# ELU between the Strassen units: the second product of one token half moves forward, the other half's parts go through DRAM

## The chip, the core and the metric

The kernel runs on one core of a Trainium2 chip. The core has a matrix engine (PE, with its weight loader PEld), a vector engine (DVE), a scalar engine (ACT), a general engine (POOL) and a queue that issues DMAs (SP). Each engine works through its own list of instructions in order; an instruction waits until the semaphores it needs are set. The metric is the device time of one execution in microseconds (us), the median of several.

## The reference

Three stages follow each other. Batch 4, 8 heads, 576 positions, width 64 give 2304 tokens of 512 numbers, all in float32.

```python
out = attention_on_4x_pooled_rows(q, k, v)      # repeated four times along the sequence
out += attention_in_a_band(q, k, v)             # |i - j| < 4
x = out as 2304 x 512
h = x @ w_in                                    # 512 x 2048
g = np.where(h > 0, h, np.exp(np.minimum(h, 0)) - 1)   # ELU
x = g @ w_out                                   # 2048 x 512
a = x @ w_gate                                  # 512 x 1536
y = (a / (1 + np.exp(-a))) * (x @ w_val)        # x @ w_val: 512 x 1536
return y @ w_o2                                 # 1536 x 512
```

## The kernel before

Every float32 operand of a large product is split into a leading part and a rest ("hi" and "lo"); `products` then runs three matmuls (hi by hi, hi by lo, lo by hi), lines 994 to 996. The hi part is an ACT copy (line 1178), the lo part a subtraction on DVE or POOL (line 1175); `split_into` adds both.

The first MLP takes 1440 tokens in five chunks of 288 directly. The last 864 tokens are two halves of 432, and their first product is written with the seven products of a Strassen (Winograd) scheme, in 8 *units* (one per 256 of the 2048 columns). A unit is 7 products of 6 matmuls of 432 columns: 42 matmuls. `add_seven` keeps three PSUM banks (Z, E, B) for a unit; ACT copies four results out (line 1204), DVE adds three more to those copies (line 1207), and a later product of the unit accumulates in a bank only after its copy. A unit yields the 256 columns of h for both halves.

`add_last` runs this part. Before the change it works in two passes. First all 8 units: the results of a unit (`De`, `Do`, named `blk`) are stored to DRAM (`yd1`, line 1356). Then, for each half and each pair of column blocks, they are loaded again (`y`, line 1369), put through ELU (negative part on ACT or DVE, lines 1374 and 1376; exponential on ACT, line 1379; minus one and maximum on DVE, line 1380), split, and multiplied by `w_out`: 12 matmuls of 432 columns per 128 columns, 24 per unit and half. The four accumulators of a half hold four PSUM banks.

The weights of a unit are built by `add_weight_unit`: four sums of blocks and up to eight splits. Its buffers are `wu` (two of them, each as large as a whole unit) or, for every third unit of the first MLP, four small ones (`wt`). The second MLP (`add_second`) has the same units with 512 columns, three token groups and two kinds (`gate`, `val`) for six pairs of column blocks; its POOL also multiplies gate by value (`blk`), and prepares the weights of the last product (`add_output_weights`: tiles `t`, `oh`, stored to `od`).

The order of the program is not written out. A planner (`Work`) gets each step with its engines, its cost, what it reads and writes, and a due time; it plays the engines in time and lets each free engine take the ready step that is due first. Most numbers in the class-like block of constants are due times or offsets of due times. A step emitted is fixed: the engines then follow that order, whatever the real durations are.

Of the kernel before, what the change touches and what calls it, by code (L numbers as in the profile page):

```python
# [9 lines left out]
F32 = mybir.dt.float32  # L10
F32R = mybir.dt.float32r
# [3 lines left out]
AF = mybir.ActivationFunctionType  # L15
# [121 lines left out]
class Work:  # L137
# [5 lines left out]
    SECOND = 34.88  # L143
# [158 lines left out]
def attention_moe_moe(ctx: ExitStack, tc: tile.TileContext, q, k, v, w_in, w_out, w_gate, w_val, w_o2, ident_in, mask_in, band_in, picks_in, out):  # L302
# [80 lines left out]
    STEP2 = 7.62  # L383
    START = 37.63
    STEP0 = 4.81
    STEP = 4.49
    FIRST = -40.0
    VALUES = -46.28
    LATER = 113.73
    POOLED = -0.58  # L390
    EARLY = 3.56
    PREFER = -31.24
    EAGER = 27.32
    URGENT = 26.59
    FREE = 21.5
    SLACK = 0.0
    LOAD = 32.85
    KEEP0 = 2.05
    KEEP1 = 4.5
    DIRECT = 2, 3, 1  # L400
    PARTS1 = 32.94
    UNIT1 = -3.64
    LAG1 = 4.87
    PARTS = 10.49
    OUT = -4.36
    SUMS = 12.13
    SUMS3 = 2.56
    SECOND2 = 15.47
    LATE = 54.53
    AWAY0 = 2.17  # L410
    AWAY1 = 5.67
    LO1 = 16.02
    HI1 = 5.93
    LO2 = 26.91
    HI2 = 34.0
    LO3 = 32.37
    HI3 = 34.82
    KEYS = 29.3
    POOL1 = -0.72
    POOL0 = 19.72  # L420
    POOL2 = 10.16
    LOCAL = 3.95
    ROWS = 20.24
    INPUT = -2.49
# [43 lines left out]
    def add_words(due, raw, u, reads=()):  # L468

        def size():  # L470
            nc.scalar.activation(u.t.bitcast(F32), raw.t[:, :, 1].bitcast(F32), AF.Prelu, scale=2.0 ** -BIAS, alpha=MINUS)

        def rest():
            nc.scalar.activation(raw.t[:, :, 0], raw.t[:, :, 0].bitcast(U32), AF.Copy, bias=TOP3[1], scale=TOP3[0])

        def words():
            t = u.t.bitcast(I32)
            nc.vector.scalar_tensor_tensor(
                out=t, in0=t, scalar=3, op0=ALU.logical_shift_left, in1=raw.t[:, :, 0], op1=ALU.bitwise_or)
# [3 lines left out]
        return add("dve", 0.64, due - 2.5, words, reads=[raw, u, *reads], writes=[u])  # L483

    def add_weights(keys, dues, whole):

        made = {}
        for n, key in enumerate(keys):
# [18 lines left out]
            low = add(("act", "dve"), (0.67, 0.7), due - 4, rest, reads=[raw, w.whole], writes=[w], second=3.0)  # L507
# [660 lines left out]
    def both_cost(engines, n):  # L1168
        return tuple(0.16 + n * 0.00104 if e == "dve" else 0.06 + n * 0.0023 for e in engines)
# [60 lines left out]
    def add_direct(key, due, to, buf, after, more=()):  # L1230
# [18 lines left out]
        add("dve", 1.18, due - 2.5, words, reads=[raw, buf], writes=[buf])  # L1249
# [15 lines left out]
    def add_weight_unit(kind, j, due, after, whole):  # L1265

        engines = EITHER if kind == "in" else PO
        u, s, w = gens.new([P, 4, HT], name="u"), gens.new([P, 4, HT], name="s"), Unit(kind == "in" and j % 3 == 2)
# [27 lines left out]
    PROD1 = 6 * 0.1964  # L1296
# [21 lines left out]
    def add_last(opened, exps, closed, made):  # L1318
# [20 lines left out]
        yd1 = [pools["dram"].tile([P, 2, TS], F32, tag=f"y1_{j}", name="yd1") for j in range(NJ1)]  # L1339
        ws, stored_h, after, pes1 = [], {}, opened, []  # L1340
        for j in range(NJ1):
            start = base + 7 * PROD1 * j
# [3 lines left out]
            De, Do = (gens.new([P, 2, HS], name="blk") for _ in range(2))  # L1346

            def emit(m, ps, first, w=w):
                a = AT[m]
                for k in range(2):  # L1350
# [4 lines left out]
                             [(De, 0), (De, 1), (Do, 0), (Do, 1)], HS, None, w)  # L1355
            stored_h[j] = [add("sp", 0.5, start + 7 * PROD1 + 2, lambda j=j, par=par, D=D: nc.sync.dma_start(
                out=yd1[j][:, par], in_=D.t.rearrange("p h c -> p (h c)")), reads=[D], after=[*done[2 * par], *done[2 * par + 1]], nbytes=P * TS * 4)
                for par, D in ((0, De), (1, Do))]
            pes1.append([t for x2 in xs.values() for b in x2 for t in b.readers if "pe" in t.costs][-7:])
        base += 7 * PROD1 * NJ1  # L1360
        ran = []
        for h in range(2):
            acc = [banks.new(lambda: range(8)) for _ in range(NP)]
            after2 = []
            for j in range(NJ1):
                due = base + 24 * 0.1964 * (j + NJ1 * h)
                Y, E = (gens.new([P, 2, HS], name="y1") for _ in range(2))
                gs = [slot(h_slots) for _ in range(2)]
                add("sp", 0.5, due - 12 - LAG1, lambda j=j, h=h, Y=Y: nc.sync.dma_start(out=Y.t, in_=yd1[j][:, :, h * HS:(h + 1) * HS]),
                    writes=[Y, E], nbytes=P * 2 * HS * 4, after=[*stored_h[j], *(ran[-4] if len(ran) > 3 else pes1[(-3, -2, -2, -1)[len(ran)]])])  # L1370

                def negative(engine, Y=Y, E=E):
                    if engine == "act":
                        nc.scalar.activation(E.t, Y.t, AF.Relu, scale=-1.0)
                    else:
                        nc.vector.tensor_scalar(out=E.t, in0=Y.t, scalar1=-1.0, scalar2=0.0, op0=ALU.mult, op1=ALU.max)  # L1376

                add(COPIER, (0.92, 1.0), due - 8 - LAG1, negative, reads=[Y], writes=[E], second=3)
                last_exp = [add("act", 0.92, due - 7 - LAG1, lambda E=E: nc.scalar.activation(E.t, E.t, AF.Exp, scale=-1.0), reads=[E], writes=[E])]
                add("dve", 1.06, due - 6 - LAG1, lambda Y=Y, E=E: nc.vector.scalar_tensor_tensor(  # L1380
                    out=Y.t, in0=E.t, scalar=-1.0, op0=ALU.add, in1=Y.t, op1=ALU.max), reads=[Y, E], writes=[Y])
                for par, g in enumerate(gs):
                    split_into(EITHER, due - 5 - LAG1, lambda g=g: g.t[:, 0], lambda g=g: g.t[:, 1], lambda Y=Y, par=par: Y.t[:, par], [Y], [g], [g], HS)

                    def gemm2s(h=h, j=j, par=par, g=g, acc=acc):
                        wo = wt["out", 2 * j + par]
                        if (h, j, par) == (1, NJ1 - 1, 1):
                            over.append(1)
                        for i in range(NP):
                            cs = slice(i * P, (i + 1) * P)  # L1390
                            products(acc[i].t[:, :HS], (wo.t[:, 0, cs], wo.t[:, 1, cs]), (g.t[:, 0], g.t[:, 1]), j + par == 0, j + par == NJ1)

                    n = 2 * j + par
                    after2.append(add("pe", 12 * 0.1964, due + 2.36 * par, gemm2s, reads=[wt["out", n], g], writes=acc,
                                      after=after2[-1:] if n == NF1 - 1 else [*after2[:1], *after2[-2:-1]]))
                ran.append(after2[-1:])
            x2s = pools["dram"].tile([P, NP, HS], F32, tag=f"x2_{NC + h}", name="x2d")
            put = []
            for i in range(NP):
                t = gens.new([P, HS], name="o1")  # L1400
                add(COPIER, (0.55, 0.6), due + 5, lambda engine, i=i, t=t, acc=acc: copy(engine, t.t, acc[i].t[:, :HS]), reads=[acc[i]], writes=[t], second=0)
                put.append(add("sp", 0.5, due + 6, lambda i=i, t=t, x2s=x2s: nc.sync.dma_start(out=x2s[:, i], in_=t.t), reads=[t], nbytes=P * HS * 4))
            segments.append((TP + h * HS, TP + (h + 1) * HS, x2s, put))
        return last_exp, [*ws[-1].made.values()], pes1[-1], base + 2 * NF1 * 12 * 0.1964
# [31 lines left out]
    def add_second(opened, exps, closed, base, behind):  # L1436
        xs, tokens = {}, {}
        for g, (t0, T) in enumerate(groups):
# [3 lines left out]
            for h, (s0, n) in enumerate(halves):  # L1442
                pieces = [(max(s0, a) - s0, min(s0 + n, z) - s0, x[:, :, max(s0, a) - a:min(s0 + n, z) - a], made)
                          for a, z, x, made in segments if a < s0 + n and z > s0]
                for kh in range(2):
                    raw = raws[kh, h] = slot(raw_slots, 4)

                    def load(kh=kh, pieces=pieces, raw=raw):
                        for a, z, x, _ in pieces:
                            nc.sync.dma_start(out=raw.t[:, :, a:z], in_=x[:, 2 * kh:2 * kh + 2])  # L1450

                    add("sp", 1.0, due - 6, load, writes=[raw], nbytes=P * 2 * n * 4,
                        after=[*opened, *(t for *_, made in pieces for t in made)])
# [37 lines left out]
        for u in units:  # L1491
# [3 lines left out]
            if n == len(ws):  # L1495
                ws.append(add_weight_unit(kind, j, start - (14.0 if j else 9.0 if kind == "gate" else 8.0), [*ws[-1].made.values()] if n > 1 else behind, 1 in gs_of[n]))
            w, x = ws[n], xs[g]
            mults = DV if j == 0 else PO
# [73 lines left out]
        for j in range(NJ):  # L1572
            after = add_output_weights(j, base + 2.0 + j, after)
            put += after
        wos = {m: [] for m in ORDER7}
        for i, m in enumerate(ORDER7):
            for jp in range(NJ // 2):
# [6 lines left out]
                add("sp", 1.0, end - 36 + 2 * i, load, writes=[x], nbytes=P * 4096, after=[*put, *(pes[NJ - 1, "val", 0] if i < 4 else pes[NJ - 2, "gate", 2])])  # L1584
# [3 lines left out]
        for q, (t, g) in enumerate(pairs_b):  # L1588
# [3 lines left out]
            for jp in range(NJ // 2):  # L1592
                raw = raws[0 if whole else jp]
                add("sp", 0.5, start - (14 if whole else 30) + jp, lambda jp=jp, t=t, raw=raw, whole=whole: nc.sync.dma_start(
# [5 lines left out]
            for i, raw in enumerate(raws):  # L1600
# [8 lines left out]
                early = 10 if whole else 14  # L1609
# [187 lines left out]
```

## Time and profile before

| | us |
|---|---|
| median of 3 runs | 964.13 (963.45 to 966.09) |
| profiled execution | 968.46 |
| its span, first to last instruction | 966.4 |
| PE busy in it | 923.7 (96%) |
| DVE, ACT, POOL busy | 582.1, 507.5, 571.4 |

The profile is one execution. A matmul overlaps the next one, so the busy time of PE is the time in which at least one runs; what is left of the span is time in which PE waits. "PEclk" is the granted clock as a share of the full one.

### The profile page before, as it was taken

Reading aid. Unit: us, or ns where it says so; the run is one execution under the profiler, and the core shown is the slowest. Engines: PE = TensorE matmul, PEld = TensorE weight load, DVE = VectorE, ACT = ScalarE, POOL = GpSimd, SP = SyncE. Lnnn points to the kernel's source line nnn. Section 1 sums busy time; section 2 is a strip of 40 time slices with the busy share of each in tenths; the row PEclk is TensorE's granted clock in tenths of the full one; section 3 lists DMA queues with packets and bytes.
Section 4 is the critical chain, followed back from the end, with each engine's and each line's share of the span. In section 5 each row is a group of like instructions: output and inputs, shape, how many; then the busy total and the mean of one; then the engine's idle time right before and its main releaser. Section 6 shows DMA issues by size and latency. Waiting matters only on the chain.

```text
span 966.4 us, 20022 instructions
## 1 busy us (share of the span) xinstructions
PE 923.7 (96%) x7573; PEld 833.3 (86%) x7573; DVE 582.1 (60%) x939; ACT 507.5 (53%) x1096; POOL 571.4 (59%) x639
## 2 busy tenths in 40 slices
PE   9679999999999999999889899999999999999998
PEld 8567889998989999999778788777888887899998
DVE  2898877666677466224577886554332223986773
ACT  3678756454455456335465566746543425444541
POOL 4778855766665764156978625999887939100000
PEclk9999999999999999999999999999999999999999
DMA  5898635778844764488937236563313269943331
GB/s 152 293 253 270 105 105 141 124 247 266 145 127 130 232 212 134 170 271 287 287 110 241 96 135 221 206 241 109 142 45 119 99 222 300 316 156 119 124 127 44
DMA packets 196752, 172.12 MB, mean 178 GB/s; under 512 B 96176, under 2 KB 170288, under 8 KB 196656
## 3 DMA queue, kind: packets, MB, share of 16 engines
q1 hardware_dynamic: 196512, 170.58, 57.4%
q8 instruction: 60, 0.98, 0.4%
q14 instruction: 36, 0.29, 0.1%
q10 hardware_dynamic: 144, 0.26, 0.1%
HBM read 111.62 MB, written 59.18 MB: 177 GB/s over the span
## 4 chain that ended last, share of the span: by engine, by line
PE 71%; DVE 10%; POOL 7%; DMA 5%; ACT 3%; issue 3%; SPq 1%; POOLq 0%; ACTq 0%; DVEq 0%
PE bank L994 22%; PE bank L996 21%; PE bank L995 21%; PE bank L1028 2%; PE bank L693 1%; PE bank L624 1%; POOL oh L1175 1%; POOL wu L1175 1%; DMA wd<-mid 1%; DVE u L1243 1%; DMA w<-in_k_dram 1%; DMA y<-yd 1%; DVE y L1376 1%; POOL t L1175 1%; PE bank L893 1%
## 5 line engine op out<-in xcount | busy, mean ns | idle before, releaser
L1207 DVE TENSOR_TENSOR blk<-bank,blk 128x512 f32<-128x512 f32 (+1 forms) x96 | 64.1, 669 | 141.6 <-PE bank L996 119.0
L994 PE MATMUL bank<-xs,wu 128*128 128x512 f32 x336 | 133.6, 398 | 5.2 <-ACT o L352 2.3
L996 PE MATMUL bank<-xs,wu 128*128 128x512 f32 x336 | 133.5, 397 | 0.8 <-POOL wu L1175 0.8
L995 PE MATMUL bank<-xs,wu 128*128 128x512 f32 x336 | 133.2, 396 | 0.0
L1204 ACT COPY blk<-bank 128x512 f32<-128x512 f32 (+1 forms) x104 | 58.5, 565 | 109.0 <-PE bank L996 104.7
L994 PE MATMUL bank<-os,ys 128*128 128x256 f32 x378 | 107.3, 284 | 1.9 <-DVE o L1207 1.0
L996 PE MATMUL bank<-os,ys 128*128 128x256 f32 x378 | 107.0, 283 | 0.0
L995 PE MATMUL bank<-os,ys 128*128 128x256 f32 x378 | 106.9, 283 | 0.0
L994 PE MATMUL bank<-x,w 128*128 128x288 f32 x320 | 100.7, 315 | 2.9 <-DVE g L1035 1.4
L995 PE MATMUL bank<-x,w 128*128 128x288 f32 x320 | 95.4, 298 | 0.2 <-POOL x L982 0.2
L996 PE MATMUL bank<-x,w 128*128 128x288 f32 x320 | 95.0, 297 | 0.0
L1079 POOL TENSOR_TENSOR g<-e,g 128x288 fp32r<-128x288 f32 x64 | 53.8, 841 | 54.0 <-ACT g L352 39.2
L994 PEld LDWEIGHTS bank<-xs,wu 128*128 128x128 f32 x336 | 63.3, 188 | 21.3 <-DVE blk L1207 3.0
L996 PEld LDWEIGHTS bank<-xs,wu 128*128 128x128 f32 x336 | 63.2, 188 | 17.4 <-POOL wu L1175 2.3
L994 PE MATMUL bank<-g,w 128*128 128x288 f32 x256 | 77.9, 304 | 0.0
L995 PE MATMUL bank<-g,w 128*128 128x288 f32 x256 | 75.5, 295 | 0.0
L995 PEld LDWEIGHTS bank<-xs,wu 128*128 128x128 f32 x336 | 63.3, 188 | 14.1
L996 PE MATMUL bank<-g,w 128*128 128x288 f32 x256 | 75.4, 294 | 0.0
L994 PEld LDWEIGHTS bank<-os,ys 128*128 128x128 f32 x378 | 72.5, 192 | 2.7 <-DVE o L1207 1.4
L995 PEld LDWEIGHTS bank<-os,ys 128*128 128x128 f32 x378 | 72.5, 192 | 0.0
L996 PEld LDWEIGHTS bank<-os,ys 128*128 128x128 f32 x378 | 72.5, 192 | 0.0
L1175 POOL TENSOR_TENSOR wu<-s,wu 128x256 fp32r<-128x256 f32 x78 | 57.8, 769 | 17.8 <-ACT wu L1178 17.7
(220 smaller groups left out, 2620.4 us busy)
## 6 DMA issues: line engine op xcount, KB each, us to landing
yr<-yd SPq DMA_DIRECT2D x27, 512.0 KB
yd<-blk SPq DMA_DIRECT2D x24, 512.0 KB
os<-od SPq DMA_DIRECT2D x42, 256.0 KB
w<-in_moe_w_in_dram SPq DMA_DIRECT2D x16, 512.0 KB
w<-in_moe_w_out_dram SPq DMA_DIRECT2D x16, 512.0 KB
wp<-w SPq DMA_DIRECT2D x16, 512.0 KB
u<-wd SPq DMA_DIRECT2D x32, 256.0 KB
wd<-mid SPq DMA_DIRECT2D x56, 128.0 KB
```

The lines of the kernel that those rows point to most:

```text
L624: nc.tensor.matmul(sc[j].t[s * QB:(s + 1) * QB, (u * NP + p) * QB:(u * NP + p + 1) * QB], parts["qT"][p].t[j * D:(j + 1) * D, a:a + QB], p ...
L693: nc.tensor.matmul(pvs[u].t[j * D:(j + 1) * D, p * U:(p + 1) * U], tvs[u].t[:, (2 * p + j) * D:(2 * p + j + 1) * D], bd.t[:, u, j * NP + p ...
L893: nc.tensor.matmul(sc[0].t[j * D:(j + 1) * D, 2 * G:3 * G], vs0.t[:, w, j], prT0.t[:, j, w], start=(w == 0), stop=(w == 1))
L994: nc.tensor.matmul(ps, sh, mh, start=first, stop=False, skip_group_check=more)
L995: nc.tensor.matmul(ps, sh, ml, start=False, stop=False, skip_group_check=more)
L996: nc.tensor.matmul(ps, sl, mh, start=False, stop=last, skip_group_check=more)
L1028: nc.tensor.matmul(acc[0][i].t[:, :T1], wo.t[:, i * P:(i + 1) * P].bitcast(F32), ge(), start=f == 0, stop=f == NF1 - 1)
L1079: add("pool", 0.86, due - URGENT, lambda e=e, g=g: nc.gpsimd.tensor_tensor(out=g.t[:, 1], in0=e.t, in1=g.t[:, 0], op=ALU.subtract), reads= ...
L1175: return task(engines, n, due, lambda engine=engines[0]: two(engine).tensor_tensor(out=out(), in0=in0(), in1=in1(), op=op), reads, writes, ...
L1204: return add("act", ps_copy, when(m) - 20, lambda: nc.scalar.copy(d(i), ps.t[:, :w]), reads=[ps], writes=of(i))
L1207: return add("dve", ps_sum, when(m) - 20, lambda: nc.vector.tensor_tensor(out=d(i), in0=ps.t[:, :w], in1=d(i), op=ALU.add), reads=[ps], wr ...
L1243: nc.vector.scalar_tensor_tensor(out=t, in0=t, scalar=3, op0=ALU.logical_shift_left, in1=pairs(raw.t)[:, :, 0], op1=ALU.bitwise_or)
```

## The change

- ELU and the splits of a unit follow the unit at once, from SBUF (`y1`), first for half 1 and then for half 0. The negative part is always on ACT. The constants ELU1 and ELU0 are their offsets.
- The second product of half 1 runs on PE between the units, two units later (LAGG). Its parts `g1` stay in SBUF.
- The parts of half 0 are stored to DRAM (`gd`) and loaded back by the half's second products, which run after the last unit. At most DEPTH (6) loads run ahead; the first six wait until the seven products of the last unit are done.
- The results of a unit no longer go through DRAM before ELU. The count and size of transfers is the same: 16 stores and 16 loads of 432 KB.
- All weight units use the two `wu` buffers; the small `wt` ones are gone (`Unit(False)`).
- Preparing the last product's weights is due from 63.35 us after the first MLP on, each of six 26.72 us later than the one before; till now the six were due at once, 2 us after it.
- In the last two pairs of the second MLP the weights and multiplications of the third token group go to DVE alone (`tail`).
- The planner's costs of some steps are other numbers, and nearly all due times are.

The matmuls are the same in number and shape.

```diff
-        engines = EITHER if kind == "in" else PO
-        u, s, w = ..., Unit(kind == "in" and j % 3 == 2)
+        engines = EITHER if kind == "in" else DV if tail else PO
+        u, s, w = ..., Unit(False)
...
+        def gemms(h, j, par, g, due):
+            ...
+            done.append(add("pe", 12 * PROD2, due, gemm2s, reads=[wt["out", n], g], writes=acc, after=...))
...
-            De, Do = (gens.new([P, 2, HS], name="blk") for _ in range(2))
+            Y = [gens.new([P, 2, HS], name="y1") for _ in range(2)]
...
-            stored_h[j] = [add("sp", 0.5, ..., nc.sync.dma_start(out=yd1[j][:, par], in_=D.t ...
+            for h in (1, 0):
+                y, E = Y[h], gens.new([P, 2, HS], name="e1")
+                due = start + 7 * PROD1 + (ELU1 if h else ELU0)
+                add("act", 0.92, due, ... AF.Relu, scale=-1.0 ..., holds=[y], after=[*done[h], *done[2 + h]])
+                exp = add("act", 0.92, due + 1, ... AF.Exp, scale=-1.0 ...)
+                add("dve", 1.06, due + 2, ... scalar_tensor_tensor ..., port=DV)
+                for par in range(2):
+                    g = gens.new([P, 2, HS], F32R, name="g1")
+                    split_into(EITHER, due + 3, ...)
+                    if h:
+                        gemms(h, j, par, g, start + pace * LAGG + PROD1 * 7 + 12 * PROD2 * par)
+                    else:
+                        put_g[j].append(add("sp", 0.5, due + 5, ... dma_start(out=gd[j][:, par], in_=g.t ...
...
+                add("sp", 0.5, due - 12, ... dma_start(out=g.t, in_=gd[j][:, par]), writes=[g],
+                    after=[*put_g[j], *(ran[0][-DEPTH:1 - DEPTH] if len(ran[0]) >= DEPTH else pes1[-1])])
+                gemms(0, j, par, g, due)
...
-            after = add_output_weights(j, base + 2.0 + j, after)
+            after = add_output_weights(j, base + O2A + O2B * j, after)
...
-        return tuple(0.16 + n * 0.00104 if e == "dve" else 0.06 + n * 0.0023 for e in engines)
+        return tuple(0.16 + n * 0.00104 if e == "dve" else 0.18 + n * 0.0022 for e in engines)
```

What this does to the order shows first on ACT. Before, in the pass over the units, ACT holds the copies of products out of PSUM (`blk<-bank`) and the hi parts of the next unit's weights (`wu<-s`):

```order
L1204 COPY blk_5966<-bank_5996 128x432
L1204 COPY blk_6032<-bank_6031 128x432
L1204 COPY blk_6098<-bank_6097 128x432
L1178 CAST wu_6084<-s_6058 128x256 x4
L1204 COPY blk_6099<-bank_6119 128x432
L1204 COPY blk_6033<-bank_6031 128x432
```

After, at the second unit, the negative part and exponential of the first unit (`e1`, line 1405 and 1406) and its hi parts (`g1`) stand between those copies (`y1<-bank`, line 1219):

```order
L1405 ACTIVATE e1_5954<-y1_5807 128x864
L1219 COPY y1_5945<-bank_5944 128x432
L1406 ACTIVATE e1_5954<-e1_5954 128x864
L1219 COPY y1_5806<-bank_5805 128x432
L1219 COPY y1_5946<-bank_5964 128x432
L1193 CAST wu_5971<-s_5838 128x256
L1193 CAST g1_5998<-y1_5807 128x432
L1193 CAST g1_6002<-y1_5807 128x432
L1405 ACTIVATE e1_6005<-y1_5806 128x864
L1219 COPY y1_5946<-bank_5944 128x432
```

So a copy that PE needs (the last row) now stands behind an activation of 864 columns and behind hi parts that need DVE's result.

The second place is POOL where the second products begin. Before, the lo parts for them (`xh`) stand among the sums and splits of the second MLP's first weights (`s`, `wu`):

```order
L1175 TENSOR_TENSOR xh_6452<-y1_6371,xh_6452 128x432
L1175 TENSOR_TENSOR xh_6463<-y1_6371,xh_6463 128x432
L1175 TENSOR_TENSOR s_6438<-u_6437 128x256 x2
L1175 TENSOR_TENSOR s_6438<-s_6438,u_6437 128x256
L1175 TENSOR_TENSOR wu_6492<-u_6437,wu_6492 128x256
L1175 TENSOR_TENSOR s_6438<-u_6437,s_6438 128x256
L1175 TENSOR_TENSOR wu_6492<-u_6437,wu_6492 128x256 x2
L1175 TENSOR_TENSOR wu_6492<-s_6438,wu_6492 128x256 x3
L1175 TENSOR_TENSOR xh_6542<-y1_6449,xh_6542 128x432
L1175 TENSOR_TENSOR xh_6545<-y1_6449,xh_6545 128x432
```

After, at the end of the last unit, four lo parts of the seventh unit stand in a row, and the weights of the second MLP behind them:

```order
L1190 TENSOR_TENSOR g1_6687<-y1_6520,g1_6687 128x432
L1190 TENSOR_TENSOR g1_6690<-y1_6520,g1_6690 128x432
L1190 TENSOR_TENSOR g1_6738<-y1_6519,g1_6738 128x432
L1190 TENSOR_TENSOR g1_6740<-y1_6519,g1_6740 128x432
L1190 TENSOR_TENSOR s_6702<-u_6701 128x256 x2
L1190 TENSOR_TENSOR s_6702<-s_6702,u_6701 128x256
L1190 TENSOR_TENSOR wu_6753<-u_6701,wu_6753 128x256
L1190 TENSOR_TENSOR s_6702<-u_6701,s_6702 128x256
L1190 TENSOR_TENSOR wu_6753<-u_6701,wu_6753 128x256 x2
L1190 TENSOR_TENSOR wu_6753<-s_6702,wu_6753 128x256 x4
```

PE's second products read these lo parts. Of the four in the list before, two stand behind eight or more rows of the second MLP's weights; in the list after, all four stand ahead of those weights.

## Rows read from the trace of the kernel before

**Rows 1.** Stages: start:end and length, each engine's busy us, clock, DMA.
```profile
0.00:381.00 381.00, 360.74 (x4372) 329.75 (x4373) 267.10 (x536) 220.52 (x531) 252.35 (x313) 1.00 0.68 184
381.00:458.00 77.00, 77.00 (x410) 73.66 (x409) 22.97 (x38) 32.60 (x76) 36.61 (x48) 1.00 0.70 235
458.00:551.00 93.00, 79.68 (x378) 72.88 (x376) 66.73 (x51) 54.53 (x99) 75.69 (x68) 0.96 0.55 178
551.00:824.00 273.00, 269.23 (x1287) 221.00 (x1288) 124.81 (x170) 139.68 (x288) 205.94 (x212) 1.00 0.49 172
824.00:966.40 142.40, 137.03 (x1134) 136.02 (x1132) 100.50 (x146) 60.16 (x104) 0.81 (x1) 1.00 0.43 144
```

**Rows 2.** Who PE waited for, 458 to 552: us, times, longest.
```profile
PE bank L995 <- POOL xh L1175: 8.6, 6, 4.4
PE bank L994 <- ACT xh L1178: 2.4, 1, 2.4
PE bank L994 <- ACT o L352: 2.3, 1, 2.3
```

**Rows 3.** Timeline of PE: start, us, instruction, idle before it and releaser.
```profile
439.85 0.36 PE L994 MATMUL bank<-xh,wt 128*128 128x432 f32 x1
...
458.75 0.36 PE L994 MATMUL bank<-xh,w 128*128 128x432 f32 x1
463.52 0.46 PE L995 MATMUL bank<-xh,w 128*128 128x432 f32 x1 [4.41 <-POOL xh L1175]
```

**Rows 4.** The chain that ended last: start us, us, what.
```profile
458.45 3.96 POOL wu L1175 x4
462.41 1.06 POOL xh L1175
471.00 5.28 DMA y<-yd
...
512.27 4.86 DMA y<-yd
```

**Rows 5.** Timeline of DVE at two places.
```profile
476.38 6.96 DVE L1376 TENSOR_SCALAR y<-y 128x864 f32<-128x864 f32 x1 [8.58 <-DMA y<-yd]
...
643.25 5.41 DVE L1243 SCALAR_TENSOR_TENSOR u<-u,r 128x512 int32<-128x512 int32 x1
```

**Rows 6.** Timeline of POOL, where the first of these two ends.
```profile
481.44 1.43 POOL L1175 TENSOR_TENSOR wu<-u,wu 128x256 fp32r<-128x256 f32 x2
```

**Rows 7.** Timeline of PE, behind the second of them.
```profile
649.32 0.50 PE L994 MATMUL bank<-xs,wu 128*128 128x512 f32 x1 [1.24 <-DVE blk L1531]
```

**Rows 8.** Instruction groups by shape, 381 to 551: busy us, mean ns, idle before.
```profile
L1175 POOL TENSOR_TENSOR xh<-y,xh 128x432 fp32r<-128x432 f32 x32 | 43.3, 1378 | 18.5 <-ACT xh L1178 18.5
L1380 DVE SCALAR_TENSOR_TENSOR y<-y,y 128x864 f32<-128x864 f32 x16 | 25.2, 1589 | 9.0 <-ACT y L1379 9.0
L1204 ACT COPY blk<-bank 128x432 f32<-128x432 f32 x32 | 16.6, 518 | 38.5 <-PE bank L996 36.4 <-issue 1.4 <-DVE blk L1207 0.7
L1178 ACT CAST xh<-y 128x432 fp32r<-128x432 f32 x32 | 16.1, 552 | 14.4 <-DVE y L1380 10.0 <-PE bank L996 4.2
L1379 ACT ACTIVATE y<-y 128x864 f32<-128x864 f32 x16 | 14.8, 924 | 11.2 <-DVE y L1376 11.2
L1178 ACT CAST wu<-s 128x256 fp32r<-128x256 f32 x24 | 8.7, 404 | 0.8 <-POOL s L1175 0.8
```

**Rows 9.** POOL's groups by shape, 560 to 840.
```profile
L1175 POOL TENSOR_TENSOR wu<-s,wu 128x256 fp32r<-128x256 f32 x48 | 35.6, 769 | 0.2 <-ACT wu L1178 0.2
...
L1175 POOL TENSOR_TENSOR blk<-blk,sg 128x1024 f32<-128x1024 f32 x10 | 24.1, 2411 | 13.5 <-ACT sg L1520 13.5
...
L1175 POOL TENSOR_TENSOR blk<-blk 128x512 f32<-128x512 f32 x10 | 13.6, 1358 | 0.0
L1175 POOL TENSOR_TENSOR oh<-t,oh 128x512 fp32r<-128x512 f32 x8 | 10.6, 1349 | 1.8 <-issue 1.8
...
L1175 POOL TENSOR_TENSOR t<-u 128x256 f32<-128x256 f32 x8 | 7.1, 894 | 15.5 <-DVE u L1243 14.8 <-POOL blk L1175 0.7
```

More of the change, by code (lines that the diff above doesn't have):

```diff
@@ L142 @@
     LATENCY = 0.15
-    SECOND = 34.88
+    SECOND = 89.22
     CHANGE = 0.15
@@ L379, in bank @@
         return banks.new(lambda: places)
[L383 to L386, printed above, removed]
+    STEP2 = 8.09
+    START = 41.55
+    STEP0 = 4.34
+    STEP = 4.83
     FIRST = -40.0
[L388 to L395, printed above, removed]
+    VALUES = -63.27
+    LATER = 175.53
+    POOLED = -2.91
+    EARLY = 1.57
+    PREFER = -29.95
+    EAGER = 31.73
+    URGENT = 18.77
+    FREE = 15.19
     SLACK = 0.0
-    LOAD = 32.85
-    KEEP0 = 2.05
-    KEEP1 = 4.5
+    LOAD = 40.9
+    KEEP0 = 3.51
+    KEEP1 = 2.3
     DIRECT = 2, 3, 1
[L401 to L424, printed above, removed]
+    PARTS1 = 41.73
+    UNIT1 = -1.54
+    LAGG = 2
+    TAILW = True
+    WOS0 = 41.69
+    WOS1 = -0.01
+    EARLYA = 19.9
+    EARLYB = 10.69
+    LOADA = 42.74
+    LOADB = 23.91
+    O2A = 63.35
+    O2B = 26.72
+    ELU1 = 11.45
+    ELU0 = 21.5
+    UNIT2 = 23.72
+    UNIT0 = 6.38
+    RAW = 12.6
+    DEPTH = 6
+    PARTS = 18.37
+    OUT = -5.99
+    SUMS = 4.25
+    SUMS3 = 2.48
+    SECOND2 = 14.93
+    LATE = 63.08
+    AWAY0 = 2.23
+    AWAY1 = 6.42
+    LO1 = 15.64
+    HI1 = 15.39
+    LO2 = 29.1
+    HI2 = 25.91
+    LO3 = 30.57
+    HI3 = 27.72
+    KEYS = 23.4
+    POOL1 = -2.95
+    POOL0 = -0.71
+    POOL2 = 12.89
+    LOCAL = 0.73
+    ROWS = 15.21
+    INPUT = -8.79
     order = [(c, f) for c in range(NC) for f in range(NF1)]
@@ L482, in add_words @@
         add("act", 0.43, due - 4, size, reads=[raw, *reads], writes=[u])
-        return add("dve", 0.64, due - 2.5, words, reads=[raw, u, *reads], writes=[u])
+        return add("dve", 0.5, due - 2.5, words, reads=[raw, u, *reads], writes=[u])
     def add_weights(keys, dues, whole):
@@ L506, in add_weights @@
             add("sp", 0.5, due - LOAD, lambda key=key, raw=raw: load_w(key, raw.t), writes=[raw], nbytes=P * 4096)
-            low = add(("act", "dve"), (0.67, 0.7), due - 4, rest, reads=[raw, w.whole], writes=[w], second=3.0)
+            low = add(("act", "dve"), (0.67, 0.5), due - 4, rest, reads=[raw, w.whole], writes=[w], second=3.0)
             add("act", 0.64, due - 3.5, size, reads=[raw], writes=[ps], after=[low])
@@ L1248, in add_direct @@
         add("act", 0.64, due - 4, size, reads=[raw], writes=[buf])
-        add("dve", 1.18, due - 2.5, words, reads=[raw, buf], writes=[buf])
+        add("dve", 0.8, due - 2.5, words, reads=[raw, buf], writes=[buf])
     class Unit:
@@ L1354, in add_last @@
             done = add_seven(lambda m, start=start: start + PROD1 * SLOT7[m], PROD1, emit, lambda m: xs[m],
[L1355 to L1358, printed above, removed]
+                             [(Y[0], 0), (Y[1], 0), (Y[0], 1), (Y[1], 1)], HS, None, w)
@@ L1359, in add_last @@
             pes1.append([t for x2 in xs.values() for b in x2 for t in b.readers if "pe" in t.costs][-7:])
[L1360 to L1374, printed above, removed]
-                    else:
[L1376 to L1403, printed above, removed]
@@ new lines, in add_last @@
+        base += pace * (NJ1 + LAGG)
+        put_out(1, base)
+        for j in range(NJ1):
+            for par in range(2):
+                g = slot(h_slots)
+                due = base + 12 * PROD2 * (2 * j + par)
+                add("sp", 0.5, due - 12, lambda j=j, par=par, g=g: nc.sync.dma_start(out=g.t.bitcast(F32), in_=gd[j][:, par]), writes=[g],
+                    nbytes=P * 2 * HS * 4, after=[*put_g[j], *(ran[0][-DEPTH:1 - DEPTH] if len(ran[0]) >= DEPTH else pes1[-1])])
+                gemms(0, j, par, g, due)
@@ L1495, in add_second @@
             if n == len(ws):
-                ws.append(add_weight_unit(kind, j, start - (14.0 if j else 9.0 if kind == "gate" else 8.0), [*ws[-1].made.values()] if n > 1 else behind, 1 in gs_of[n]))
+                ws.append(add_weight_unit(kind, j, start - (UNIT2 if j else UNIT0), [*ws[-1].made.values()] if n > 1 else behind, 1 in gs_of[n], TAILW and gs_of[n] == (2,) and j >= NJ - 2))
             w, x = ws[n], xs[g]
-            mults = DV if j == 0 else PO
+            tail = g == 2 and j >= NJ - 2
+            mults = DV if j == 0 or tail else PO
             if T > HT:
```

55 lines of the change are left out of this document (44 added, 11 removed).

## The prediction

> **What bounds the kernel now.** I read the table of stages first [rows 1]. The five stretches are the reader's map: attention and the first MLP's direct chunks (0 to 381), the Strassen units of the first MLP (381 to 458), its second products for the two halves (458 to 551), the second MLP (551 to 824), the last product and the end. PE is busy 360.7, 77.0, 79.7, 269.2 and 137.0 us in them, so it waits 20.3, 0, 13.3, 3.8 and 5.4 us. The sum of these, 42.7 of 966.4 us, is all that a new order can win, and the dense place to win it is the third stretch: a wait of 14% there, against 0 and 1% in its neighbours.
>
> Next I asked whom PE waits for there [rows 2]: POOL's lo parts (`xh`) for 8.6 us in six waits, an ACT hi part for 2.4, an ACT copy of attention (`o`) for 2.3. That is 13.3, all of it. PE's timeline has the longest wait, 4.41 us ahead of 463.52 [rows 3]; the chain of waits says why [rows 4]: POOL did four splits of the second MLP's weights (3.96 us from 458.45) and only then the lo part (1.06). So it is POOL's queue, and not a transfer or PE, that sets the end. The other links there are loads `y` (5.28 and 4.86 us), in the chain since POOL has to wait for ACT's and DVE's work behind each load.
>
> The clock column of that stretch is 0.96 [rows 1]; elsewhere it is 1.00. Full is 2.4 GHz; part of the stretch ran at the lower level, 1.2. A mean of 0.96 over 93.0 us means 7.4 us at that level, and so 0.04 × 93.0 = 3.7 us of work lost; I take 3.5, since the 0.96 is rounded.
>
> **The change, part by part.**
>
> *The waits of the second products go.* In the pass over the units there is nothing to wait for: ACT is busy 32.6 of 77 us, DVE 23.0, POOL 36.6 [rows 1]. In the next 93 us the work piles up: DVE 66.7, ACT 54.5, POOL 75.7. The change lays the two beside each other: 16 ELUs and 64 splits go over 170 us. POOL's load falls from 75.7 of 93 (81%) to (36.6 + 75.7)/170 = 66%. In the order the lo parts of the last units stand ahead of the second MLP's weights on POOL. I count the 13.3 us of waiting and the 3.5 us of clock as gone: −16.8.
>
> *What it costs in units 2 and 3.* One matmul of 432 columns takes 0.197 us: (458.75 − 439.85)/96 [rows 3], with 96 matmuls between the two rows. A unit without a second product lasts 42 × 0.197 = 8.27 us on PE, one with a half's second product 66 × 0.197 = 13.0. The second product starts two units late, so two units have no cover by it. Per unit ACT has 4 copies at 0.518, 4 hi parts at 0.552, two exponentials at 0.924, two negative parts at about the same, and 4 hi parts of weights at 0.404 [rows 8]: 2.07 + 2.21 + 1.85 + 1.85 + 1.62 = 9.6 us. That is 1.3 us over PE's 8.27, twice 2.7 over two units at most; 0 if part of it is pushed into later units, where 13.0 − 9.6 = 3.4 us are free. Between 0 and 2.7 I take 1.0, nearer to 0, since the splits may go to three engines. In the other units ACT has room, and POOL as well: 12 sums and splits at 0.769 [rows 9] and at most two lo parts at 1.378 [rows 8] are 12.0 of 13.0 us.
>
> *Two weight buffers where there were six.* A unit's loads now wait for the last product of the unit two before. Ahead of unit 3 that leaves a second product of 24 matmuls as cover, 24 × 0.197 = 4.7 us, and a little more ahead of unit 4. Sums, hi and lo parts must follow. It is a wait of 0 where the parts come in the order in which the seven products use them, and of 1.2 us if one split (1.16 us, ACT 0.404 + POOL 0.769) is late. I take 0.5.
>
> *Half 0 through DRAM.* Its first loads wait for the last unit's products. They are covered by half 1's last second product, 4.7 us, against landing times of 5.28 and 4.86 us for a load of the same size [rows 4]. Late by 0 to 0.6 us, twice that with a queue behind the first: 0 to 1.2, I take 0.5. Then PE eats a load each 2.4 us with six ahead, 14 us: covered.
>
> *In-order queues.* The evictions that free PSUM for a unit now stand behind activations and hi parts that wait for DVE, as ACT's list shows. The same stretch of 142 us (8 units of 8.27 and 16 second products of 4.7) had no wait in its first part [rows 1], and 13.3 per 93 in its second. The ends are 0 and 142 × 13.3/93 = 20. I take 3.0, nearer to 0: an eviction queued behind one activation is late by 0.924 us, and each unit has two banks to work on meanwhile.
>
> *Relu off DVE.* It is 6.96 us for 864 columns on DVE at 476.38 [rows 5], where the neighbouring operation of the same size has a mean of 1.589 [rows 8]; it ends at 483.3, as POOL's row of 1.43 from 481.44 ends at 482.87 [rows 6]. So DVE stood still until POOL paused. With the relu on ACT this goes, and is part of the −16.8 (POOL's lo parts wait for it by way of ACT's exponential).
>
> *Second MLP.* PE waits 3.8 us there. Spreading the last product's weights over the pairs adds POOL work to each: per pair two weight units, 2 × 12 × 0.769 = 18.5, multiplications 4 × 2.411 + 4 × 1.358 = 15.1, and every 26.72 us a set of 5 × 0.894 + 3 × 1.349 = 8.5 us, that is 8.5 × 44.9/26.72 = 14.3 per pair [rows 9]. That is 47.9 at most, against PE's 269.2/6 = 44.9 [rows 1]: POOL falls behind by up to 3 us per pair where all three meet, in pairs 1 to 3, at most 9; less, as the weights start 23.72 us ahead, where it was 14. The last two pairs get DVE's help. Ends: −2 (half of the 3.8 goes) to +7.5. I take +1.5.
>
> By the Trainium skill, "SBUF — State Buffer", section "Who interferes with whom", VectorE and GpSimd share a port pair under an exclusive lock that one instruction holds to its end. The trace agrees: the 6.96 us above, and a DVE operation of `words` that took 5.41 us [rows 5] with a wait of PE of 1.24 us behind it [rows 7]. By that rule a change that makes POOL busier in the second MLP blocks DVE there, which speaks against this change. It stands below as a rival.
>
> *The rest.* 0 to 381 and 824 to the end keep their work. Nearly all due times are other numbers, so the waits of 20.3 and 5.4 us are dealt anew: 0, with ±3.
>
> The sum: −16.8 + 1.0 + 0.5 + 0.5 + 3.0 + 1.5 = −10.3 us. The profiled execution is 968.46; 958.2 comes out. It was 4.33 over the median, so the median is predicted at 953.8, 954.
>
> **Rivals.**
>
> *All of it goes.* The units and second products run like 381 to 458, with no wait, and the second MLP loses nothing: −16.8, 947. For: PE's two units of slack, free engines. Against: ACT's 9.6 on 8.27.
>
> *POOL becomes the bound of the second MLP.* It loses 7.5 us by the sums above, and DVE operations held up as that of 5.41 us was, two or three more of them, cost PE 1.24 each, some 3: 954 + (7.5 − 1.5) + 2 to 3 = 962. For: 47.9 on 44.9, and [rows 5, 7]. Against: POOL is busy 205.9 of 273 there now, with the last product's weights in it [rows 1], so 67 us are free; and the weights start earlier.
>
> *ACT's queue holds up PE between the units (the other side).* The units' copies wait behind hi parts, these for DVE's maximum, that for ACT's exponential; PE waits for the copies and DVE for PE's banks. It happens in all eight units. From 16.8/8 = 2.1 us a unit on, the change gives back all it wins. At 3 us a unit, the length of copy, negative part, exponential and hi part in one row (0.518 + 0.924 + 0.924 + 0.552 = 2.9), it is 24: 964 − 16.8 + 24 = 971. Against: 3.4 us of ACT free per unit, half of the ELU due 11 and 21 us behind its unit.
>
> That the change doesn't do what it says is excluded by the orders: the lists are the program.
>
> **How the numbers follow.** Forecast 954: 0.53. All goes, 947: 0.12. POOL, 962: 0.17. ACT's queue, 971: 0.13. Another loss or gain in 0 to 381 beyond 3 us: 0.05, half of it slower. The forecast's own range is 948 to 960, from the terms' ends taken two at a time (−16.8 to −4). The range for 8 in 10 reaches from 944 (947 and the 3 us of the rest) to 968, which takes in POOL's case and leaves out ACT's. Within 0.3%, about what a measurement of this kernel can tell from no change, is 961.2 to 967.0. Faster: 0.53 × 0.95 + 0.12 + 0.17 × 0.4 and 0.01 = 0.70. Same: the rest of POOL's, of the forecast's, and 0.02 each of ACT's and the last: 0.16. Slower: 0.14.
>
> **What would show it.** Right: a stretch of some 172 us from the first unit to the last second product with waits of PE under 6 us; clock 1.00 in it; no DVE operation of 864 columns at 7 us; POOL's `t` and `oh` spread over five pairs. ACT's term: PE waits for ACT `y1` in units 2 and 3. DRAM: a wait for a load `g` at the first second product of half 0. Second MLP: waits for POOL `wu` or DVE `u` around the `t` rows. The forecast is wrong if PE waits for `y1` or `g1` in each unit, or if 0 to 381 moves by more than 3 us.

## The result and the profile after

| | before | after |
|---|---|---|
| median, same chip | 963.79 (963.42 to 966.09, 4 runs) | 940.41 (939.44 to 941.33, 4 runs) |
| ratio, 95% interval | | 0.9752 (0.9732 to 0.9773) |
| profiled execution, its span | 968.46, 966.4 | 939.44, 937.6 |

The change took off 23.4 us. Forecast were 954 and a range of 944 to 968: the direction is right, the size is not, and the time lies below the range.

To compare stages I cut both executions at the same events: the first matmul of a unit, the end of the last second product, the end of the second MLP. The windows view of before at these cuts (columns as in [rows 1]):

```profile
0.00:381.40 381.40, 361.14 (x4375) 330.15 (x4376) 267.10 (x536) 220.65 (x532) 252.35 (x313) 1.00 0.68 184
381.40:547.20 165.80, 154.79 (x777) 145.28 (x776) 87.69 (x86) 85.82 (x171) 109.23 (x112) 0.98 0.63 206
547.20:823.90 276.70, 270.62 (x1292) 221.77 (x1292) 126.71 (x173) 140.85 (x290) 208.91 (x215) 1.00 0.49 171
823.90:966.40 142.50, 137.12 (x1135) 136.12 (x1133) 100.60 (x146) 60.16 (x104) 0.91 (x1) 1.00 0.43 144
```

and of after:

```profile
0.00:374.60 374.60, 353.92 (x4375) 324.43 (x4376) 263.58 (x525) 221.56 (x533) 246.03 (x306) 0.95 0.69 184
374.60:525.80 151.20, 151.20 (x783) 144.01 (x782) 66.57 (x76) 91.42 (x179) 105.29 (x122) 1.00 0.61 213
525.80:803.00 277.20, 274.63 (x1341) 227.73 (x1340) 145.01 (x221) 148.99 (x311) 183.11 (x190) 1.00 0.56 192
803.00:937.60 134.60, 130.06 (x1080) 129.44 (x1078) 94.94 (x126) 56.26 (x92) 0.00 (x0) 1.00 0.40 134
```

- Units and second products: 165.8 to 151.2, −14.6. PE waited 11.0 us there (165.80 − 154.79) and now not at all: busy 151.20 of 151.20, clock 1.00. The other 3.6 is the clock (0.02 × 165.8 = 3.3) and matmuls that last longer behind a wait (0.46 against 0.36, [rows 3]).
- The second MLP and the end: 419.2 to 411.8, −7.4. Here the two rows belong together, since some 50 matmuls moved from the last row to the third. Waits fell from 6.1 + 5.4 to 2.6 + 4.5, that is 4.4. The other 3.0 is busy time; 6 more matmuls in the stretch of the units (783 against 777) take 1.4 of it at 0.23 each, the rest I can't place.
- Ahead of the units: 381.4 to 374.6, −6.8, with 20.3 us of waits before and 20.7 after. After's clock of 0.95 there comes mostly from 20 to 60 us, where it is 0.54 (the lower level, 1.2 GHz, for the most part) and PE is busy 26.06 of 40 us. It cost nothing that shows: with the negative part done twice (below), PE has the same order up to the first unit and a clock of 1.00 from 20 to 60 us, and reaches that unit at 375.3. So the 0.95 can't be read as a loss of 0.05 × 374.6 us.

The three make 28.8, the medians only 23.4. Part of the first stretch is the execution that was profiled. Three of the experiments below have before's PE instructions up to the first unit, in the same order; with before itself they reach the unit at 381.4, 381.2, 378.5 and 376.2, mean 379.3. After and the seven of its variants that have its PE order up to there reach it at 374.6 to 376.3, mean 375.4. So 3.9 us are left of the 6.8, and the rest is scatter. That the new due times make these 3.9 is not shown: after with before's due times (below) reaches the unit at 376.0, only 0.6 later.

Of what PE waited for between the units and behind them [rows 2] nothing is left. All of PE's waits of after that are over 1.1 us (us, times, longest):

```profile
PE bank L811 <- DVE nm L819: 8.0, 1, 8.0
PE bank L639 <- issue: 3.6, 2, 1.9
PE bank L639 <- DVE w L657: 1.4, 2, 1.1
PE bank L1009 <- DVE blk L1588: 1.3, 1, 1.3
PE bank L1009 <- DVE blk L1222: 1.2, 2, 1.1
PE bank L1009 <- DVE e L1087: 1.2, 2, 0.7
PE warm L1691 <- DVE bd L1686: 1.2, 1, 1.2
```

The first three are attention's, in the first 60 us. No `y1`, `g1`, `gd` or `wu` is among them.

### The profile page after: what moved, and what is told of

The parts are those of the page before. It is cut to its first block, busy times and chain, and to the rows that moved or that the text cites. A ratio compares the mean times of both kernels' runs of the same rounds, so it can differ in the third digit from the quotient of the medians.

```text
span 937.6 us, 19981 instructions
## 1 busy us (share of the span) xinstructions
PE 909.8 (97%) x7573; PEld 825.6 (88%) x7573; DVE 570.1 (61%) x946; ACT 518.2 (55%) x1112; POOL 534.4 (57%) x617
## 5 line engine op out<-in xcount | busy, mean ns | idle before, releaser
L1009 PE MATMUL bank<-g,w 128*128 128x288 f32 (+1 forms) x320 | 100.9, 315 | 0.0
L1010 PE MATMUL bank<-g,w 128*128 128x288 f32 (+1 forms) x320 | 98.6, 308 | 0.0
L1011 PE MATMUL bank<-g,w 128*128 128x288 f32 (+1 forms) x320 | 98.5, 308 | 0.0
L1222 DVE TENSOR_TENSOR blk<-bank,blk 128x512 f32<-128x512 f32 x72 | 49.4, 689 | 75.5 <-PE bank L1011 70.4
L1219 ACT COPY blk<-bank 128x512 f32<-128x512 f32 x72 | 42.1, 584 | 73.4 <-PE bank L1011 69.0
```

Source lines behind the costliest of these rows:

```text
L1009: nc.tensor.matmul(ps, sh, mh, start=first, stop=False, skip_group_check=more)
L1010: nc.tensor.matmul(ps, sh, ml, start=False, stop=False, skip_group_check=more)
L1011: nc.tensor.matmul(ps, sl, mh, start=False, stop=last, skip_group_check=more)
L1219: return add("act", ps_copy, when(m) - 20, lambda: nc.scalar.copy(d(i), ps.t[:, :w]), reads=[ps], writes=of(i))
L1222: return add("dve", ps_sum, when(m) - 20, lambda: nc.vector.tensor_tensor(out=d(i), in0=ps.t[:, :w], in1=d(i), op=ALU.add), reads=[ps], wr ...
```

## The experiments

Four theories, as the expectations name them. A: PE waited because lo parts stood behind weights on POOL. B: it waited because POOL held up DVE's relu. C: the new due times made the gain. D: there was too much ELU and split work beside too little PE work, whatever its order.

**Lo parts ahead of the weights, in the kernel before.** It now waits with the second MLP's first weights for the first half's lo parts:

```diff
+                if h == 0:
+                    first_parts += [t for g in gs for t in g.writers]
...
-        return last_exp, [*ws[-1].made.values()], pes1[-1], ...
+        return last_exp, [*ws[-1].made.values(), *first_parts], pes1[-1], ...
```

> The kernel before, with one edit: the first weights of the second MLP also wait for the lo parts of the first half that loads y again. POOL then does those lo parts ahead of the weights. Theory A (PE waited in its second products because the lo parts stood behind the second MLP's weights in POOL's queue): the 8.6 us of waits for POOL's xh fall under 2 and the clock stays at 1.00, so 964 - 8 to - 12 = 952 to 956. Theory B (PE waited because POOL held up DVE's relu): the relus of 7 us remain, and so do most waits, 961 to 965. Theory C (the new due times elsewhere made the gain): 961 to 966.

970.29, ratio 1.0052 (1.0034 to 1.0071): 0.5% slower. PE's waits from 380 to 560:

```profile
PE bank L995 <- POOL xh L1175: 6.8, 4, 3.5
PE bank L995 <- DVE xs L1175: 0.9, 1, 0.9
PE bank L994 <- ACT o L352: 0.5, 1, 0.5
```

8.6 us became 6.8. In the first half, whose lo parts now stand ahead, 0.7 is left of it; 6.2 are in the other half, whose lo parts still stand among weights. The units and second products last 161.1 us and not 165.8, but waits in the second MLP rose from 6.1 to 11.1 us as its weights came later. So POOL's order decides where PE waits, and the work put back costs more than it gave: theory A does not stand as a cause by itself. An order with both halves' lo parts ahead was not run.

**Relu on ACT alone, in the kernel before.**

```diff
-                add(COPIER, (0.92, 1.0), due - 8 - LAG1, negative, reads=[Y], writes=[E], second=3)
+                add(("act",), (0.92,), due - 8 - LAG1, lambda negative=negative: negative("act"), reads=[Y], writes=[E])
```

> The kernel before, with the negative part of ELU always on ACT (12 of 16 stood on DVE). The lo parts keep their place behind the weights on POOL. Theory B (POOL holding up DVE's relu): no DVE operation of 864 columns over 3 us but the maximum, and half of the waits for xh gone, 955 to 959. Theory A (POOL's queue order): the wait of 4.41 us stays, the time within 3 us of 964. Theory C: as A.

965.93, ratio 0.9999 (0.9982 to 1.0016): no change. The waits, 375 to 560:

```profile
PE bank L995 <- POOL xh L1175: 7.1, 5, 2.7
PE bank L994 <- ACT xh L1178: 2.1, 2, 1.1
```

The relus on DVE, the longest of them 7 us [rows 5], are gone, the waits are not. Theory B falls.

**Only the due times: the constants that both kernels have, swapped.** There are 39 of them (the expectation says 38).

```diff
-    START = 37.63
+    START = 41.55
...
```

> The kernel before, with the 38 constants that both kernels have set to the values of the kernel after (due times of the attention, of the direct chunks and of the weights); the ELU stays in its own pass. Theory C (part of the gain is due times alone): the waits of 20.3 us ahead of the first Strassen unit fall by some 5 and the time by 5 to 9, 955 to 959, while the waits of the second products stay. Theories A and B: 961 to 967, since they put the whole gain at the second products.

978.74, ratio 1.0123 (1.0084 to 1.0162): slower by some 13 us, which no theory expected. The first unit starts at 374.7, as in after, but the units and second products last 176.6 us against 165.8. Due times set for one structure can cost that much in another.

> The kernel after, with the same 38 constants set back to the values of the kernel before; ELU between the units, the DRAM way of half 0 and the later weights of the last product stay. Theory C: the first unit starts some 5 us later and the time is 945 to 950. Theories A and B: within 3 us of 940. In each the stretch of units and second products stays without waits of PE.

946.60, ratio 0.9799 (0.9768 to 0.9829). Against after's 0.9752 the due times give 0.5%, 4.5 us, and only with the structure that they were set for. The expectation had the place wrong: the first unit starts at 376.0, not some 5 us later. From the windows view, the units and second products, the second MLP and the end:

```profile
376.00:527.50 151.50, 151.50 (x783) 143.99 (x782) 56.43 (x72) 91.31 (x175) 101.74 (x115) 1.00 0.61 211
527.50:799.50 272.00, 268.58 (x1284) 220.63 (x1283) 140.78 (x208) 146.46 (x302) 183.31 (x190) 1.00 0.54 189
799.50:945.20 145.70, 138.08 (x1135) 137.67 (x1134) 99.56 (x138) 59.83 (x102) 0.00 (x0) 0.99 0.41 136
```

So with before's due times the structure still has no wait in the units. What they cost lies behind: 417.7 us from there to the end, where after has 411.8, with 11.0 us of waits against 7.1. Theory C holds for about a fifth of the gain, and not where it put it.

**No second product between the units.** In the kernel after, half 1's parts are stored and loaded like half 0's, and its second products follow the last unit:

```diff
-                    if h:
-                        gemms(h, j, par, g, start + pace * LAGG + ...)
-                    else:
-                        put_g[j].append(add("sp", 0.5, due + 5, ...
+                    put_g[h, j].append(add("sp", 0.5, due + 5, ...
...
-        for j in range(NJ1):
+        for h in (1, 0):
+            for j in range(NJ1):
```

> The kernel after, with the parts of both halves sent through DRAM: ELU and splits still follow each unit, but no second product runs between the units; all 16 of them follow the last unit. Theory D (what counts is how much PE work lies beside the ELU and the splits; neither the place of the lo parts on POOL nor the relu on DVE alone): the eight units have 66 us of PE work for 8 x 9.6 = 77 us on ACT, and as much as 12 sums and splits at 0.763 and four lo parts at 1.155 = 13.8 us a unit on POOL where DVE takes none of them, so PE waits 10 to 25 us in the units: 950 to 965. Theory E (what counts is that the results no longer go through DRAM ahead of ELU, so that second products read finished parts): no waits, within 3 us of 940.

967.80, ratio 1.0044 (1.0025 to 1.0064). It gives back the whole gain, 27.4 us. The stretch and PE's waits in it:

```profile
374.70:556.20 181.50, 163.87 (x800) 147.77 (x800) 65.77 (x80) 101.87 (x198) 126.23 (x138) 0.98 0.80 287
```

```profile
PE bank L1009 <- DVE y L1222: 5.8, 6, 1.1
PE bank L1009 <- ACT wu L1193: 5.2, 5, 1.2
PE bank L1009 <- ACT e L1405: 2.9, 1, 2.9
PE bank L1009 <- DMA xh<-gd: 1.8, 3, 1.0
PE bank L1011 <- POOL wu L1190: 1.4, 4, 0.9
PE bank L1009 <- DMA wu<-wp: 0.4, 1, 0.4
```

17.6 us of waits (181.50 − 163.87), for DVE, ACT, POOL and loads alike. 4.7 of them, the two rows of 2.9 and 1.8, are at second products; the others are in the units, where POOL is full from 420 to 458:

```profile
420.00:458.00 38.00, 28.53 (x131) 23.24 (x129) 12.95 (x17) 27.33 (x56) 37.59 (x40) 1.00 0.75 266
```

ELU between the units is no gain if PE has only a unit's 8.27 us to lay over it. This is what theory D expected: in before the second products were overfull, here the units are, and in after neither is. Theory E, no waits, falls. Due times other than the pace were not set anew for this order, and it moves twice as many parts through DRAM; how much of the 27.4 us either holds was not tested.

**Less lag.** `LAGG = 2` became `LAGG = 0`.

> The kernel after, with half 1's second product due behind its own unit and not two units later (LAGG 0); in the order it starts after 72 unit matmuls, where it was 114. Theory D: the work beside PE is nearly the same, ELU and split of a unit need 0.93 + 0.93 + 1.3 + 0.55 + 1.16 = 4.9 us behind its copies, and 30 matmuls of the next unit cover 5.9 us: within 3 us of 940. If the two units of lag are what keeps PE from waiting, PE waits 1 to 5 us at each of eight units: 948 to 980.

943.82, ratio 0.9791 (0.9775 to 0.9807): 3.4 us later than after, a little more than theory D's 3. The stretch has 1.4 of it in the profiled execution (152.6 against 151.2), and PE's only wait there is 0.9 us for a load `xh<-gd`. The lag is not what keeps PE from waiting.

**More work on ACT.** In the kernel after, each negative part is done twice, and four times. The order on the other engines is word for word the same, so this adds load alone.

```diff
-                ... lambda y=y, E=E: nc.scalar.activation(E.t, y.t, AF.Relu, scale=-1.0), writes=[E] ...
+                ... lambda y=y, E=E: [nc.scalar.activation(E.t, y.t, AF.Relu, scale=-1.0) for _ in range(4)][-1], writes=[E] ...
```

> The kernel after, with each negative part of ELU done twice on ACT (16 activations of 864 columns more, 0.927 us each; the order on the other engines is the same). ACT's sum per unit goes from 9.6 to 11.4 us, under the 13.0 us that PE needs with a second product. Theory F (ACT's load counts only above PE's): within 2 us of 940. Theory G (a copy out of PSUM behind an activation delays PE by its length): 2 x 0.927 x 8 = 15 us, 950 to 957.

941.14, ratio 0.9752 (0.9722 to 0.9782): 0.7 us more than after, within the noise, for 14.8 us more of ACT.

> The kernel after, with each negative part done four times (48 activations more, 44.5 us of ACT; other engines' order the same). ACT's sum per unit is 15.2 us, over PE's 13.0. Theory F: (15.2 - 13.0) x 8 = 17 us at most, less by what the lag of two units and the stretch behind the units cover: 945 to 958, with PE waiting for y1 or g1. Theory G: 44 us, 975 to 988.

970.69, ratio 1.0053 (1.0034 to 1.0071): 30 us more, for 44.5 us of ACT. The two stretches, twice and then four times:

```profile
375.30:528.20 152.90, 151.99 (x783) 143.66 (x782) 57.91 (x76) 106.01 (x195) 106.73 (x122) 1.00 0.61 210
```

```profile
375.80:558.20 182.40, 162.77 (x783) 147.91 (x782) 56.08 (x76) 134.36 (x227) 104.97 (x122) 0.96 0.51 176
```

and what PE waited for with four:

```profile
PE bank L1009 <- ACT y L1219: 13.5, 12, 2.8
PE bank L1009 <- ACT wu L1193: 2.7, 2, 1.5
PE bank L1010 <- POOL g L1190: 1.7, 1, 1.7
PE bank L1009 <- DVE y L1222: 1.3, 1, 1.3
PE bank L1011 <- POOL wu L1190: 0.3, 1, 0.3
```

The copies out of PSUM stand behind the activations, as the rival on ACT's queue said:

```profile
411.17 3.80 ACT L1405 ACTIVATE e<-y 128x864 f32<-128x864 f32 x4
414.87 0.50 ACT L1219 COPY y<-bank 128x432 f32<-128x432 f32 x1
```

```profile
415.43 0.47 PE L1009 MATMUL bank<-xh,wu 128*128 128x432 f32 x1 [1.65 <-ACT y L1219]
```

The copy ends at 415.37 and PE goes on at 415.43. Between 11.4 and 15.2 us of ACT per unit, against PE's 13.0, lies the point from which it counts. The loss is between theory F's 17 and G's 44: 19.6 us of waits (182.40 − 162.77), 0.04 × 182.4 = 7.3 of clock. The other 4.3 of the 31.2 us are not placed; part of it can be the first matmul behind each wait, which lasts 0.46 us or so against 0.36.

**Relu on DVE, in the kernel after.**

```diff
-                add("act", 0.92, due, lambda y=y, E=E: nc.scalar.activation(E.t, y.t, AF.Relu, scale=-1.0), writes=[E], ...
+                add("dve", 1.0, due, lambda y=y, E=E: nc.vector.tensor_scalar(out=E.t, in0=y.t, scalar1=-1.0, scalar2=0.0, ...
```

> The kernel after, with all 16 negative parts on DVE in place of ACT. Theory B (a DVE operation of 864 columns waits until POOL pauses, and PE behind it): relus of 3 to 7 us on DVE, PE waits for y1 or g1 and 948 to 960. Theory D: DVE has room (66.7 of 151 us), the lag of two units covers what POOL holds up, within 3 us of 940, with relus that last long all the same.

940.41, ratio 0.9751 (0.9734 to 0.9768): no change, and the relus are short, at most 1.15 us, where both theories expected long ones (one line's view, min/median/max in ns):

```profile
L1405 DVE TENSOR_SCALAR e<-y x16: 604/759/1148, 389.8 to 477.5; 128x864 f32<-128x864 f32 x16
```

**The last product's weights due early, in the kernel after.** `base + O2A + O2B * j` became `base + 2.0 + j`.

> The kernel after, with the weights of the last product due as before, all six from 2 us after the first MLP. If the spreading of these weights helps the second MLP (theory S), PE waits more there, as before: 3.8 against 2.6 us, and 940 + 1 to + 4. If it is a burden, as the sum of 47.9 us of POOL on 44.9 of PE said, the time falls by 1 to 5 to 935 to 939.

955.25, ratio 0.9906 (0.9892 to 0.9921): 14.8 us later, beyond both expectations. In the second MLP PE waits 12.4 us:

```profile
PE bank L1011 <- POOL wu L1190: 7.1, 3, 2.8
PE bank L1009 <- DVE blk L1222: 5.1, 5, 1.7
PE bank L1009 <- ACT wu L1193: 0.2, 1, 0.2
```

**The same weights spread, in the kernel before.** `base + 2.0 + j` became `base + 63.35 + 26.72 * j`.

> The kernel before, with one edit: the weights of the last product due as in the kernel after, from 63.35 us on and 26.72 apart. Theory S (spreading these weights is worth its 15 us wherever it stands): the waits of the second MLP, 6.1 us in this kernel, fall under 3, and with what POOL saves in the second products the time is 950 to 960. Theory T (it is worth them only with ELU between the units, where the second MLP's first weights come later on POOL): within 3 us of 964, and the waits for xh of 8.6 us stay.

960.90, ratio 0.9946 (0.9926 to 0.9966). Theory S holds in part: the second MLP waits 2.2 us and not 6.1, but the second products keep theirs:

```profile
PE bank L995 <- POOL xh L1175: 10.1, 7, 4.7
```

**No help by DVE in the last two pairs.** In the kernel after, `TAILW` is False and `tail` too.

> The kernel after, with the weights and multiplications of the third token group in the last two pairs on POOL as before, not on DVE. If POOL is late at the end of the second MLP (theory S): PE waits for POOL wu or blk in the last pair and at the first last product, 2 to 6 us, 942 to 946. If the spreading left POOL enough room: within 1 us of 940.

941.87, ratio 0.9749 (0.9725 to 0.9773): within what can be told of after. POOL had room enough.

Undone one at a time in the kernel after, the second products between the units, the spread weights and the due times cost 27.4, 14.8 and 4.5 us, together twice the gain of 23.4. They are no shares of the gain: each is worth that much only with the others in place. Alone in the kernel before, the spread weights gave 4.7 us and the due times took 13. The variants were not given due times of their own, so what they cost may hold some of that too.

## Why the prediction was wrong

By its steps, on the spans of the profiled executions, where −10.3 was forecast and −28.8 measured. Of the 18.5 us between the two, 5.0 are waits that were charged and did not come, 6.6 the second MLP and the end, 6.8 the stretch ahead of the units:

- *The waits of the second products go, −16.8.* Right: 11.0 of waits and 3.6 of busy time in the stretch, and the 2.3 us for `o` behind it, 16.9. The reason that it gave, work laid over 170 us, is the one that the runs bear out. What it read in the chain, POOL's order [rows 3, 4], and DVE's held relu [rows 5, 6] were how the crowding showed; taken away one by one they gave no gain.
- *The waits that come instead, +5.0.* This step failed. All of its four terms measured 0. The largest, 3.0 for in-order queues, was put between 0 and a rate of 13.3 per 93 us [rows 1], and that rate came from a stretch in which POOL was 81% busy. In the new stretch ACT, the fullest but POOL, is 91.4 of 151.2 us busy (60%) and POOL 105.3 (70%). The doubled relu shows how much room is left: 14.8 us more of ACT cost under 1. The prediction had the figure that decides, 3.4 us of ACT free per unit, and then charged for waits all the same. Its sum for POOL erred the other way, with at most two lo parts a unit: in after all four stand there (32 in the stretch, 36.3 us), and no wait came of that either.
- *Units 2 and 3, weight buffers, first loads.* Their sums were right and their cover was there: in after's order the first second product comes behind 114 unit matmuls, 22 us of PE (0.197 each), so the first units' ELU had time enough, and no wait for `wu` or `gd` is left.
- *The second MLP, +1.5.* This step failed too, by its sign: with the end it measured −5.1 (−7.4, of which 2.3 is the wait for `o`, counted above). The load was well forecast: 47.9 of POOL per 44.9 us of PE means full, and POOL is 141.3 of 150 us busy:

```profile
600.00:650.00 50.00, 49.82 (x243) 40.95 (x242) 22.42 (x28) 30.39 (x64) 46.43 (x51) 1.00 0.50 171
650.00:700.00 50.00, 48.68 (x239) 40.28 (x238) 24.86 (x29) 27.02 (x55) 46.46 (x48) 1.00 0.45 164
700.00:750.00 50.00, 50.00 (x251) 41.88 (x250) 15.33 (x25) 24.83 (x55) 48.43 (x55) 1.00 0.47 163
```

But PE waits 1.5 us in it. The prediction counted the spread work as added, where it was only moved: all six sets had to be done anyway, and early they stood on POOL among the first pairs' weights. Undone in after this costs 14.8 us; done alone in before it gives 4.7.
- *The rest, 0 ± 3.* Ahead of the units −6.8 in this execution and −3.9 over several, both more than the 3 us that the prediction named as a sign of being wrong. What made it stays open: before's due times alone do not bring it back.
- *From profile to median.* The prediction took 4.33 off for before's execution, which is 4.7 over the median of this comparison; after's is 1.0 under its own. The two turn the 29.0 us between the executions' times into 23.4, and they make the miss smaller (18.8 us on the executions, 13.6 on the medians); they explain none of it.

The rival in which all waits go was the nearest, at 947. It lacked the gains of the second MLP and ahead of the units, for which no case stood. The rival on ACT's queue was a true mechanism: with four negative parts the copies wait behind them and PE behind the copies. It sets in between 11.4 and 15.2 us of ACT per unit, and the kernel stands at 9.6.

## What to carry to other kernels

Where a stretch waits because its side engines are nearly full, look for a neighbouring stretch in which PE has work and they do not, and lay the two over each other; reordering inside the full stretch moves the wait about. Don't price new waits by the rate of a crowded stretch: sum each side engine per unit of PE's work, and charge little while it stays below. Here ACT at 11.4 us of PE's 13.0 cost under 1 us; other kernels were not tried. Work that must be done in any case is not a burden where it is spread, if what PE needs next is then done first.

## What was not expected of the hardware

A DVE operation beside a busy POOL can last many times its usual time, and cost nothing. In after, off the path:

```profile
490.79 8.88 DVE L1190 TENSOR_TENSOR t<-xr 128x1024 f32<-128x1024 f32 x1 [10.38 <-DMA xr<-x2d]
499.85 1.23 DVE L1190 TENSOR_TENSOR t<-xr,t 128x1024 f32<-128x1024 f32 x1 [0.19 <-DMA r<-in_moe_w_out_dram]
```

```profile
494.22 4.36 POOL L1190 TENSOR_TENSOR g<-y,g 128x432 fp32r<-128x432 f32 x4
```

Two sums of one size, 8.88 and 1.23 us; POOL's gapless run ends at 498.58, and the first sum 1.1 us later. By the Trainium skill, "SBUF — State Buffer", section "Who interferes with whom", one of the two engines holds their shared ports to the end of its instruction, and the other waits. The rows agree that DVE waits, but not that one instruction is all: beside those 8.88 us POOL's instructions last 0.7 to 1.1 us each, one behind the other. It is the same with the 6.96 us of [rows 5], beside which POOL's last 0.7 to 1.1 us too. Nor does each gapless run hold DVE: in this one, from 473.64 on, two DVE maxima of 864 columns took 1.49 and 1.60 us (at 476.00 and 478.80). What decides it stays open. A held DVE operation is a loss only if PE waits for what stands behind it.

The 256 transposes at the start, in the same order in both kernels, took 15.63 us in one execution and 11.26 in the other. The kernel after with its relu on DVE had them slow and had a span of 938.6, 1.0 us over the other: the wait for `nm` behind them was 5.9 us where it had been 8.0. The cause of the two paces stays open. The clock behind them goes with the pace: in the six profiled executions whose transposes end by 16.5 us it is 0.54 to 0.59 from 20 to 60 us, in seven of the eight others 0.93 to 1.00. In the eighth, before with its relu on ACT, it is at 0.50 from 12 us on, while they still run. Neither pace made the first unit earlier: with after's PE order it starts at 374.6 to 376.3 behind fast ones, at 375.3 to 376.2 behind slow ones.

```profile
4.29 15.63 PE L718 MATMUL bank<-ident,w 72*64 72x72 f32 x256
```

```profile
4.29 11.26 PE L733 MATMUL bank<-ident,w 72*64 72x72 f32 x256
```
